# A two-headed SSM kernel: inverse transform on row halves of TensorE, final stage on two groups at once, eight skips on VectorE, and a new order

## The chip, the cores and the metric

The kernel runs on one NeuronCore of a Trainium2 chip. The metric is the device time of one launch in microseconds (us); the median of a few runs is given. PE is TensorE (matmul), PEld its weight loads, DVE is VectorE, ACT ScalarE, POOL GpSimd, and SP the engine whose queue issues most DMAs.

## The reference

Two heads work on inputs of 2048 positions and 640 channels, and their outputs stand side by side in a 2048 x 1280 result in bf16. Head A is a diagonal complex state-space recurrence, head B a gated long convolution:

```python
# head A
Lam_bar = exp(dt * Lam); B_bar = ((Lam_bar - 1) / Lam)[:, None] * Bmat
h[t] = Lam_bar * h[t-1] + B_bar @ x[t]
y = 2 * real(h @ Cmat.T) + x * Dskip
# head B
k_shift = sum over t in 0..3 of k shifted by t, times shift_k[:, t]
kv = k_shift * v
y = irfft(rfft(pad(kv)) * rfft(pad(ssm_k)))[:S] + kv * ssm_D
out = q * y
```

## The kernel before

**Head A** splits the time axis into four interleaved phases s = 0 to 3 (`NS`) of 512 positions, and the state into five blocks j (`NT`) of 128. `pe_in` multiplies the transposed input by B and adds the preceding phase's contribution through diagonal matrices (`diagL`); its result is evicted from PSUM by `ev_in`. For phase 0, DVE turns the result by tables of angles (`tabs`), runs a real scan and turns it back. The other phases follow from it by a product and two sums (`dve_mul`, `dve_next`). `pe_proj(i, s)` then multiplies 128 states by C, in two halves of 320 output columns with ten matmuls each, and adds `x * Dskip` by three more narrow matmuls against a diagonal matrix (`diagD`). There are sixteen such blocks. ACT copies each to SBUF (`act_yo`), and SP stores it. The list `SKV` could name blocks whose skip is added on DVE instead; it is empty here.

**Head B** works on five groups G of 128 channels. Per group, four taps on PE (`pe_tap`) and a product with v give kv, which goes through DRAM to be regrouped. The filter (h) and kv are each transformed by two matmul stages (`pe_s1`, `pe_s2`) with an eviction behind each. DVE multiplies the spectra (`dve_ym`, then `dve_y`, written y in the order, in two halves). `pe_inv` takes the inverse: for each of 16 frequencies four matmuls of 128 rows, 128 columns of weights and 128 moving columns. `act_zs` evicts it to `Zs`, two transposing DMAs (`turn_z`) turn that into `Zt`, and `pe_fin` makes the final stage with 32 matmuls a group, each with a full array and 64 moving columns. `dve_ob` multiplies by q in place in `qb`, and SP stores the group. The next load of q waits for that store.

The inverse is thus one of 128 points followed by one of 16:

```python
mm(o_re, lhsT=self.H[:, 0, k1, :], rhs=yre, start=True, stop=False)
mm(o_re, lhsT=self.H[:, 2, k1, :], rhs=yim, start=False, stop=True)
mm(o_im, lhsT=self.H[:, 1, k1, :], rhs=yre, start=True, stop=False)
mm(o_im, lhsT=self.H[:, 0, k1, :], rhs=yim, start=False, stop=True)
```

**What sets the order.** `make_plan` names every piece of work with its engine and its data dependencies. The string `ORDER` lists the names in the order in which they are issued; `@n` gives the PSUM slot and `!` takes the alternative engine (an eviction on DVE instead of ACT, a load on ACT's queue instead of SP's). Each engine runs its own pieces strictly in that order, and so does each DMA queue, so a DMA that waits holds up those behind it. In the names, `inv`, `zs`, `zt`, `fin`, `ob`, `od_`, `qi` are inverse, eviction, turn, final stage, product with q, store and load of q, each with its group; `p`, `yo`, `yd` are projection, copy and store.

Of the kernel before, what the change touches and what calls it, by code (L numbers as in the profile page):

```python
# [13 lines left out]
i32 = mybir.dt.int32  # L14
# [15 lines left out]
SKV = []  # L30
# [3 lines left out]

class Plan:
# [10 lines left out]
class Kernel:  # L46


    def __init__(self, ctx, tc, out, ins):
# [16 lines left out]
        t("c26", [128, 1], i32)  # L66
# [5 lines left out]
        t("bb", [128, 128], i32)  # L72
# [12 lines left out]
        for n, k in (("r_hi", 1), ("r_a", 1), ("rm", 2), ("r_k", 32), ("m_lo", 1), ("m_k1h", 1), ("m_ri", 1), ("ccol", 4),  # L85
                     ("r_ph", 64), ("m_ph", 16), ("m_t", 16)):
            t(n, [128, k], i32)
        t("r_mask", [128, 2])
        t("m_mask", [128, 4])
        t("m_aph", [128, 16], f32)  # L90
        t("r_cv", [128, 64])
        t("m_cv", [128, 16], f32)
# [9 lines left out]
        t("Mq", [128, 16, 4])  # L102
        t("G", [128, 2, 32, 64])
        t("H", [128, 3, 16, 128])
# [20 lines left out]
        t("qb", [128, 16, 128])  # L125
# [6 lines left out]
        self.Zt = self.zz[:, 4096:8192].rearrange("p (i b) -> p i b", i=32)  # L132
# [3 lines left out]
        self.tph = [flat(n).bitcast(i32).rearrange("p (q n) -> p q n", q=2) for n in (self.qb, self.kv_st)]  # L136
# [6 lines left out]
        self.diagG = self.H[:, 2].rearrange("p a b -> p (a b)")[:, 0:3 * n * 128].rearrange("p (s j d) -> p s j d", s=3, j=n)  # L143
# [46 lines left out]
    def pool_consts2(self):  # L190
        g = self.nc.gpsimd
        one = [[0, 1]]
        g.iota(self.c30[:], pattern=one, base=2 ** 30, channel_multiplier=0)
        g.iota(self.c26[:], pattern=one, base=2 ** 26, channel_multiplier=0)
        g.iota(self.ccol[:], pattern=[[1, 4]], base=0, channel_multiplier=0)
        g.iota(self.r_k[:], pattern=[[4, 32]], base=1, channel_multiplier=0)
        for r in range(2):
            g.iota(self.rm[:, r:r + 1], pattern=one, base=2 ** 30 * (1 - 3 * r), channel_multiplier=0)
        g.iota(self.m_ph[:], pattern=[[1, 16]], base=0, channel_multiplier=0)

    def pool_consts3(self):
# [5 lines left out]
        g.iota(self.bb[:], pattern=[[1, 128]], base=0, channel_multiplier=0)  # L207
# [5 lines left out]
    def dve_consts2(self):  # L213
# [7 lines left out]
        v.tensor_scalar(out=self.m_k1h[:], in0=p, scalar1=3, scalar2=2, op0=ALU.arith_shift_right, op1=ALU.logical_shift_left)  # L221
        v.tensor_scalar(out=self.m_ri[:], in0=p, scalar1=4, scalar2=2, op0=ALU.bitwise_and, op1=ALU.logical_shift_left)
# [42 lines left out]
    def pool_phases(self):  # L265
# [5 lines left out]
        g(out=self.m_t[:], in0=self.m_ph[:], in1=b(self.m_k1h[:, 0:1], 16), op=ALU.mult)  # L271
        g(out=self.m_ph[:], in0=self.m_ph[:], in1=self.m_t[:], op=ALU.add)
        g(out=self.m_ph[:], in0=self.m_ph[:], in1=b(self.m_ri[:, 0:1], 16), op=ALU.add)
        g(out=self.m_ph[:], in0=self.m_ph[:], in1=b(self.c26[:, 0:1], 16), op=ALU.mult)

    def act_RM(self):
        self.nc.scalar.activation(out=self.r_cv[:], in_=self.r_ph[:], func=ACT.Sin, scale=SC)
        self.cos(self.m_cv[:], self.m_ph[:], self.m_aph[:])

    def dve_RM(self):  # L280
# [4 lines left out]
        v.scalar_tensor_tensor(out=self.Mq[:], in0=self.m_cv[:].rearrange("p (a o) -> p a o", o=1).to_broadcast([128, 16, 4]), scalar=1.0 / L,  # L285
                               in1=self.m_mask[:].rearrange("p (o c) -> p o c", o=1).to_broadcast([128, 16, 4]), op0=ALU.mult, op1=ALU.mult)
# [13 lines left out]
    def pool_kk(self):  # L300
        g = self.nc.gpsimd.tensor_tensor
        g(out=self.kk[:], in0=self.kk[:], in1=self.hP[:, 0:1].to_broadcast([128, 16]), op=ALU.add)
        g(out=self.bb[:], in0=self.bb[:], in1=self.c19[:, 0:1].to_broadcast([128, 128]), op=ALU.mult)

    def pool_H(self, q):
        self.nc.gpsimd.tensor_tensor(
            out=self.tph[(NT + q) % 2][:, 0].rearrange("p (a b) -> p a b", a=4),
            in0=self.kk[:, 4 * q:4 * q + 4].rearrange("p (a o) -> p a o", o=1).to_broadcast([128, 4, 128]),
            in1=self.bb[:].rearrange("p (o b) -> p o b", o=1).to_broadcast([128, 4, 128]), op=ALU.mult)

    def act_H(self, q):
        v, ks = self.tph[(NT + q) % 2].rearrange("p r (a b) -> p r a b", a=4), slice(4 * q, 4 * q + 4)
        self.nc.scalar.activation(out=self.H[:, 1, ks, :], in_=v[:, 0], func=ACT.Sin, scale=SC)
        self.cos(self.H[:, 0, ks, :], v[:, 0], v[:, 1].bitcast(f32))

    def dve_nH(self):
        self.nc.vector.tensor_scalar_mul(out=self.H[:, 2], in0=self.H[:, 1], scalar1=-1.0)
# [253 lines left out]
    def pe_proj(self, i, s, ps):  # L571
# [4 lines left out]
        for b in range(2):  # L576
# [22 lines left out]
    def dve_yo(self, i, s, n, ps):  # L599
        v = lambda a: a.rearrange("q (b n) -> q b n", b=2)  # L600
        self.nc.vector.tensor_tensor(out=v(self.yo[(NS * i + s) % NY]), in0=ps[:, :, 0:320], in1=v(self.xs[n % NX]), op=ALU.add)

    def act_yo(self, i, s, ps):
        self.nc.scalar.copy(out=self.yo[(NS * i + s) % NY].rearrange("q (b n) -> q b n", b=2), in_=ps[:, :, 0:320])  # L604

    def store_yo(self, eng, i, s):
        eng.dma_start(out=self.o2[512 * i:512 * i + 512, 0:D].rearrange("(m s) d -> s m d", s=NS)[s], in_=self.yo[(NS * i + s) % NY])
# [87 lines left out]
    def pe_inv(self, ks, ps):  # L695
        mm = self.nc.tensor.matmul
        psf = ps[:].rearrange("p a n -> p (a n)")
        for i, k1 in enumerate(ks):
            yre, yim = (self.Xs[:, k1 // 8, r, 128 * (k1 % 8):128 * (k1 % 8) + 128] for r in range(2))
            o_re, o_im = psf[:, 256 * i:256 * i + 128], psf[:, 256 * i + 128:256 * i + 256]  # L700
            mm(o_re, lhsT=self.H[:, 0, k1, :], rhs=yre, start=True, stop=False)  # L701
            mm(o_re, lhsT=self.H[:, 2, k1, :], rhs=yim, start=False, stop=True)  # L702
            mm(o_im, lhsT=self.H[:, 1, k1, :], rhs=yre, start=True, stop=False)  # L703
            mm(o_im, lhsT=self.H[:, 0, k1, :], rhs=yim, start=False, stop=True)  # L704

    def act_zs(self, ks, ps):
        self.copy(self.Zs[:, :, 2 * ks[0]:2 * ks[0] + 8, :].rearrange("p i k c -> p k i c"),
                  ps[:].rearrange("p a n -> p (a n)").rearrange("p (k i c) -> p k i c", k=8, i=32))

    def turn_z(self, hf):  # L710
        s = slice(16 * hf, 16 * hf + 16)
        self.nc.sync.dma_start_transpose(out=self.Zt[:, s, :], in_=self.Zs[:, s].rearrange("p i k c -> p i (k c)"))

    def load_q(self, eng, G):
        eng.dma_start(out=self.qb[:], in_=self.q2[:, 128 * G:128 * G + 128].rearrange("(a b) c -> b a c", b=128))

    def pe_fin(self, hf, ps):
        psf = ps[:].rearrange("p a n -> p (a n)")
        for i in range(16):
            self.nc.tensor.matmul(psf[:, 64 * i:64 * i + 64], lhsT=self.Zt[:, 16 * hf + i, :],  # L720
                                  rhs=self.Mq[:].rearrange("p a c -> p (a c)"), start=True, stop=True)

    def dve_ob(self, hf, ps):
        cs = slice(64 * hf, 64 * hf + 64)
        self.nc.vector.tensor_tensor(out=self.qb[:, :, cs].rearrange("p a (i c) -> p a i c", c=4),  # L725
                                     in0=ps[:].rearrange("p a n -> p (a n)").rearrange("p (i a c) -> p a i c", i=16, a=16),
                                     in1=self.qb[:, :, cs].rearrange("p a (i c) -> p a i c", c=4), op=ALU.mult)

    def store_ob(self, eng, G):
# [303 lines left out]
```

## Time and profile before

| | us |
|---|---|
| median of 3 runs | 201.65 (201.57 to 202.29) |
| the profiled execution | 201.36 |
| its span | 199.6 |
| busy PE, DVE, ACT, POOL | 186.4, 164.9, 153.8, 24.8 |

The span runs from the first to the last instruction of the profiled execution; 1.76 us lie around it. Busy time adds what an engine spent in instructions. Matmuls are pipelined, so their records overlap, and a matmul's share of PE is the distance between two starts (its slot) rather than its recorded length. An idle time in square brackets is followed by what ended it.

### The profile page before, as it was taken

To read this page: it belongs to the slowest core of one execution; us is meant where nothing else is said; L and a number is where in the kernel's file an instruction comes from. 1 tells how busy PE (TensorE), PEld (TensorE's weight loads), DVE (VectorE), ACT (ScalarE), POOL (GpSimd) and SP (SyncE) were. 2 spreads that over 40 slices of the span, in tenths; PEclk is the share of its full clock that TensorE was granted. 3 is DMA by queue.
4 is the path that set the end of the run, shared out by engine and by line. 5 is a ranking of instruction groups with operands and counts; after the bars stand their busy time and mean duration, and the time that the engine had idled before them with its cause. 6 is when DMAs were issued, how large, how long until landed. Compare 5 with 4: busy or idle time off the path is not lost. (4 is left out here: it accounts for less than half of the span.)

```text
span 199.6 us, 7503 instructions
## 1 busy us (share of the span) xinstructions
PE 186.4 (93%) x3328; PEld 128.3 (64%) x3340; DVE 164.9 (83%) x285; ACT 153.8 (77%) x189; POOL 24.8 (12%) x55
## 2 busy tenths in 40 slices
PE   7999999999989999999999998887999999999990
PEld 4444365544445456567777887677778887977770
DVE  5899877999999999999999999999999898420040
ACT  2499999988958998899998899799898983501321
POOL 8899561000000000000000000000000000000000
PEclk9999999999999999999999999999999999999998
DMA  4999999993586831985999786997995796597635
GB/s 112 209 221 217 207 266 214 210 192 85 90 174 163 164 50 27 240 163 86 236 188 194 121 167 126 157 254 140 194 155 150 158 164 153 126 175 176 143 130 138
DMA packets 124908, 32.61 MB, mean 163 GB/s; under 512 B 120903, under 2 KB 124236, under 8 KB 124876
## 3 DMA queue, kind: packets, MB, share of 16 engines
q1 hardware_dynamic: 124856, 32.13, 81.0%
q8 instruction: 26, 0.43, 0.9%
q14 instruction: 6, 0.05, 0.1%
q10 hardware_dynamic: 20, 0.01, 0.0%
HBM read 9.51 MB, written 7.86 MB: 87 GB/s over the span
## 5 line engine op out<-in xcount | busy, mean ns | idle before, releaser
L520 PE MATMUL ps<-xT,BT 128*128 128x512 bf16 x188 | 47.8, 381 | 0.9 <-DMA xT<-in_A_x_dram 0.3
L582 PE MATMUL ps<-Cs,hs 128*128 128x320 bf16 x240 | 36.3, 299 | 0.3 <-ACT Xs L467 0.3
L520 PEld LDWEIGHTS <-BT 128*128 128x128 bf16 x200 | 18.7, 98 | 22.6 <-issue 1.3
L604 ACT CAST BT<-ps 128x640 bf16<-128x640 f32 x16 | 10.9, 695 | 25.7 <-PE ps L587 22.7
L582 PEld LDWEIGHTS <-hs 128*128 128x128 bf16 x240 | 21.9, 98 | 7.9 <-issue 0.2
L725 DVE TENSOR_TENSOR qb<-ps,qb 128x1024 bf16<-128x1024 f32 x10 | 11.9, 1216 | 15.9 <-PE ps L720 15.9
L675 PEld LDWEIGHTS <-G 128*64 128x64 bf16 x640 | 19.1, 110 | 5.5 <-issue 4.1
L467 ACT CAST As_kv<-ps 128x1024 bf16<-128x1024 f32 x20 | 20.0, 1041 | 0.3 <-PE ps L662 0.3
L467 ACT CAST As_h<-ps 128x1024 bf16<-128x1024 f32 x20 | 19.8, 1040 | 0.0
L467 ACT CAST Hf<-ps 128x1024 bf16<-128x1024 f32 x19 | 19.3, 1042 | 0.0
L467 ACT CAST Xs<-ps 128x1024 bf16<-128x1024 f32 x19 | 18.8, 1031 | 0.0
L467 ACT CAST zz<-ps 128x1024 bf16<-128x1024 f32 x17 | 17.2, 1034 | 2.1 <-PE ps L704 2.1
L701 PE MATMUL ps<-Xs,H 128*128 128x128 bf16 x80 | 17.5, 219 | 0.9 <-ACT As_h L467 0.5
L703 PE MATMUL ps<-Xs,H 128*128 128x128 bf16 x80 | 17.5, 219 | 0.8 <-issue 0.8
L702 PE MATMUL ps<-Xs,H 128*128 128x128 bf16 x80 | 17.5, 219 | 0.4 <-DVE Xs L693 0.4
L704 PE MATMUL ps<-Xs,H 128*128 128x128 bf16 x80 | 17.5, 219 | 0.0
L693 DVE TENSOR_TENSOR Xs<-Xs,rot 128x1024 bf16<-128x1024 bf16 x20 | 12.9, 686 | 0.2
L687 DVE TENSOR_TENSOR rot<-Xs,Hf 128x2048 bf16<-128x2048 bf16 x10 | 12.2, 1220 | 0.8 <-ACT BT L604 0.5
L675 PE MATMUL ps<-As_kv,G 128*64 128x128 bf16 x320 | 11.7, 221 | 1.0 <-DVE vT L651 0.5
L688 DVE TENSOR_TENSOR Xs<-Xs,Hf 128x2048 bf16<-128x2048 bf16 x10 | 12.2, 1225 | 0.5
L675 PE MATMUL ps<-As_h,G 128*64 128x128 bf16 x320 | 11.7, 221 | 0.7 <-ACT Xs L467 0.7
L651 DVE TENSOR_TENSOR vT<-ps,vT 128x1024 bf16<-128x1024 f32 x10 | 11.9, 1213 | 0.4 <-PE ps L646 0.4
(204 smaller groups left out, 396.5 us busy)
## 6 DMA issues: line engine op xcount, KB each, us to landing
h_st<-in_B_ssm_k_dram SPq DMA_DIRECT2D x10, 256.0 KB, 4.2
kv_rows<-vT SPq DMA_DIRECT2D x5, 512.0 KB
kv_st<-kv_rows SPq DMA_DIRECT2D x10, 256.0 KB, 3.7
qb<-in_B_q_dram SPq DMA_DIRECT2D x5, 512.0 KB, 4.0
out_dram<-BT SPq DMA_DIRECT2D x16, 160.0 KB, 2.6
out_dram<-qb SPq DMA_DIRECT2D x5, 512.0 KB, 5.2
As_kv<-in_A_B_re_dram SPq DMA_DIRECT2D x3, 160.0 KB, 2.4
As_kv<-in_A_B_im_dram SPq DMA_DIRECT2D x3, 160.0 KB, 2.5
```

The source lines that it names most:

```text
L467: self.nc.scalar.copy(out=out, in_=in_)
L520: mm(o, lhsT=self.BT[:, r, k, j * 128:(j + 1) * 128], rhs=xT[:, k, :], start=(k == 0), stop=(s == 1 and k == NT - 1))
L582: mm(o[:, 0:320], lhsT=h[:, r, ts], rhs=self.Cs[:, r, j, c0:c0 + 320], start=(j == 0 and r == 0), stop=(not on_pe and j == NT - 1 and r == 1))
L651: self.nc.vector.tensor_tensor(out=self.vT[:, ts], in0=ps[:].rearrange("p a n -> p (a n)"), in1=self.vT[:, ts], op=ALU.mult)
L675: self.nc.tensor.matmul(o[64 * e:64 * e + 64, c:c + 128], lhsT=self.G[:, r, k, :], rhs=As[:, k, :], start=True, stop=True)
L687: tt(out=self.cross(), in0=X[:, ::-1, :], in1=self.Hf[:, 1:2, hs].to_broadcast([128, 2, 1024]), op=ALU.mult)
L688: tt(out=X, in0=X, in1=self.Hf[:, 0:1, hs].to_broadcast([128, 2, 1024]), op=ALU.mult)
L693: self.nc.vector.tensor_tensor(out=X[:, r, :], in0=X[:, r, :], in1=cr[:, r, :], op=ALU.add if r else ALU.subtract)
L701: mm(o_re, lhsT=self.H[:, 0, k1, :], rhs=yre, start=True, stop=False)
L702: mm(o_re, lhsT=self.H[:, 2, k1, :], rhs=yim, start=False, stop=True)
L703: mm(o_im, lhsT=self.H[:, 1, k1, :], rhs=yre, start=True, stop=False)
L704: mm(o_im, lhsT=self.H[:, 0, k1, :], rhs=yim, start=False, stop=True)
```

## The change

**Inverse.** It becomes one of 64 points followed by one of 32. A matmul uses 64 rows of the array; the upper and the lower 64 rows hold the two halves e of the spectrum and write to two PSUM banks. Real and imaginary part stand side by side in the 128 columns of weights, taken from a table `H` of three strips (-sin, cos, sin) of which two neighbours are used. There are still 64 matmuls of 128 moving columns a group. The tables take two rounds on POOL and ACT instead of four. An eviction becomes two instructions of half the size.

**Final stage.** It has two weights' halves (real, imaginary) that accumulate, 64 output rows and 128 moving columns, so two groups share a PSUM tile, one in each half of the partitions: groups 0 and 1, 2 and 3, and group 4 by itself with its channels split in two. `qb` holds 64 partitions a group, and `Zt` gets a second buffer in the place of `tabs`. For group 4, q and the output move in two DMAs with rows of 64 channels instead of 128.

**Skip.** Eight of the sixteen projection blocks leave out the three skip matmuls per half. For these SP loads x, DVE multiplies it by Dskip (`skip_x`) and adds it while copying from PSUM (`dve_yo`). The last block of the old kind, (3, 3), is split into halves with a copy and a store each.

**Order.** Two of five warm-up pieces go, and the whole string `ORDER` is new.

```diff
-SKV = []
+SKV = [(2, 1), (0, 1), (2, 0), (3, 2), (2, 3), (3, 1), (1, 1), (1, 3)]
+LAST = (3, 3)
...
     def pe_inv(self, ks, ps):
...
+        for i, k1 in enumerate(ks):
+            for r in range(2):
+                for e in range(2):
+                    rows = slice(64 * e, 64 * e + 64)
+                    y = self.Xs[rows, k1 // 8, r, 128 * (k1 % 8):128 * (k1 % 8) + 128]
+                    self.nc.tensor.matmul(ps[:, e, 128 * i:128 * i + 128], lhsT=self.H[rows, k1, 1 - r:3 - r, :].rearrange("p o n -> p (o n)"),
+                                          rhs=y, start=(r == 0), stop=(r == 1))
...
+    def act_zs(self, ks, ps):
+        for e in range(2):
+            k = 16 * e + ks[0]
+            self.copy(self.Zs[:, :, k:k + 4].rearrange("p i k c -> p k i c"), ps[:, e].rearrange("p (k i c) -> p k i c", k=4, c=4))
...
+    def pe_fin(self, G, q, ps):
         psf = ps[:].rearrange("p a n -> p (a n)")
+        for i in range(8):
+            for r in range(2):
+                for h in range(2):
+                    g, j = (0, 16 * h + 8 * q + i) if G == NG - 1 else (h, 8 * q + i)
+                    self.nc.tensor.matmul(psf[64 * h:64 * h + 64, 128 * i:128 * i + 128], lhsT=self.Zt[g][:, j, 64 * r:64 * r + 64],
+                                          rhs=self.Mq[:, r].rearrange("p a c -> p (a c)"), start=(r == 0), stop=(r == 1))
...
-    for n, (w, d) in enumerate(((2, "dc"), (2, "wm0"), (2, "bt0"), (2, "bt1"), (2, "wm3"))):
+    for n, (w, d) in enumerate(((2, "dc"), (2, "wm0"), (2, "tsk"))):
...
+        old = [f"od_{x}" for x in ([G - 2, G - 1] if last else [G - 2])] if G > 1 else Hs + [f"tab{j}" for j in J]
+        dma(f"qi{G}", "SP", 0.8 if last else 0.42, 3.9 if last else 2.9, old, lambda e, G=G: K.qo(e, G, True))
...
-lv1! pc lsk lv0! lv4 B0 pc2 dc dc3 wm0@0 lv2! zer lv3! pc3 dc2 wm1@2 B1 gp1 dsel x1 tsk@4 gp0 bt0@6 tske@4 dS0 tv@0 wm2@2 pp
+lv3! pc lv4 B1 lsk lv0 pc2 dc3 lv2 lv1! B0! dc x1 zer wm0@0 gp0 dc2 wm1@2 bt1@4 gp1 tv@6 bt0@0 be1@4 kT0 pc3 tve@6 tsk@2 be0!@0
...
```

On DVE, before, the end of its work from the last group's spectra on stands as follows; `Xs<-Xs,rot` is the second half of the spectral product (y), `zz<-ps` an eviction of the inverse, `qb<-ps,qb` a product with q:

```order
L687 TENSOR_TENSOR rot<-Xs,Hf 128x2048
L688 TENSOR_TENSOR Xs<-Xs,Hf 128x2048
L693 TENSOR_TENSOR Xs<-Xs,rot 128x1024 x2
L465 CAST zz<-ps_64 128x8x32x4
L725 TENSOR_TENSOR qb<-ps_65,qb 128x16x64
L725 TENSOR_TENSOR qb<-ps_67,qb 128x16x64
```

After, the same place on DVE, where `BT<-BT` is a skip product and `BT<-ps,BT` the addition of a skip:

```order
L691 TENSOR_TENSOR rot<-Xs,Hf 128x2048
L692 TENSOR_TENSOR Xs<-Xs,Hf 128x2048
L603 TENSOR_TENSOR BT<-ps_64,BT 128x640
L697 TENSOR_TENSOR Xs<-Xs,rot 128x1024 x2
L738 TENSOR_TENSOR qb<-ps_65,qb 128x32x32
L599 TENSOR_TENSOR BT<-BT 128x640
L738 TENSOR_TENSOR qb<-ps_64,qb 128x32x32
L599 TENSOR_TENSOR BT<-BT 128x640
L738 TENSOR_TENSOR qb<-ps_65,qb 128x32x32
L738 TENSOR_TENSOR qb<-ps_67,qb 128x32x32
```

Behind the last spectral product there stood the two products of group 3; now the four of groups 2 and 3 stand there, with skip work between and behind them.

The queue of SP near its end, before; `zz<-zz` is a turn, `qb<-in_B_q` a load of q, `out_dram<-qb` the store of a group, `out_dram<-BT` that of a projection block:

```order
L715 DMA qb<-in_B_q_dram 128x16x128
L712 DMA_TRANSPOSE zz<-zz 128x16x128 x2
L730 DMA out_dram<-qb 128x16x128
L607 DMA out_dram<-BT 128x640
L715 DMA qb<-in_B_q_dram 128x16x128
L607 DMA out_dram<-BT 128x640 x5
L730 DMA out_dram<-qb 128x16x128
```

And after, where `BT<-in_A_x` loads x for a skip:

```order
L715 DMA_TRANSPOSE zz<-zz 128x16x128
L725 DMA out_dram<-qb 64x32x128 x2
L593 DMA BT<-in_A_x_dram 128x640
L715 DMA_TRANSPOSE zz<-zz 128x16x128
L723 DMA qb<-in_B_q_dram 64x32x64 x2
L611 DMA out_dram<-BT 128x320
L611 DMA out_dram<-BT 128x640
L593 DMA BT<-in_A_x_dram 128x640
```

The last load of q has moved behind the stores of two groups, a load of x and one of group 4's turns.

234 lines of the change are left out of this document (119 added, 115 removed).

## The prediction

> **What bounds the kernel now.** I read the page's busy shares and slices first, then busy time by stage, then the chain that ended last.
>
> ```profile
> span 199.6 us, 7503 instructions
> PE 186.4 (93%) x3328; PEld 128.3 (64%) x3340; DVE 164.9 (83%) x285; ACT 153.8 (77%) x189; POOL 24.8 (12%) x55
> PE   7999999999989999999999998887999999999990
> DVE  5899877999999999999999999999999898420040
> ```
>
> PE is full almost from first to last slice; DVE is as full until about 165 us and then has nearly nothing to do. The answer by stages (length, then busy time of PE, PEld, DVE, ACT, POOL) says it in numbers:
>
> ```profile
> 30.00:60.00 30.00, 29.20 (x431) 14.91 (x424) 28.41 (x46) 25.33 (x32) 0.78 (x1) 1.00 0.86 161
> 60.00:90.00 30.00, 29.26 (x550) 17.48 (x547) 29.25 (x43) 27.37 (x30) 0.00 (x0) 1.00 0.63 133
> 90.00:120.00 30.00, 29.26 (x710) 23.55 (x704) 29.48 (x51) 28.00 (x32) 0.00 (x0) 1.00 0.89 165
> 120.00:150.00 30.00, 26.61 (x787) 22.02 (x782) 29.38 (x44) 27.80 (x31) 0.00 (x0) 1.00 0.95 172
> 173.00:191.00 18.00, 18.00 (x166) 13.49 (x164) 3.02 (x3) 2.73 (x5) 0.00 (x0) 1.00 0.74 154
> ```
>
> From 60 to 150 us DVE is idle 0.75 + 0.52 + 0.62 = 1.9 us of 90, and PE 0.74 + 0.74 + 3.39 = 4.9 us. So two engines bind there together, DVE a little harder. From 173 us PE alone works, on projection blocks that were left over. The seam is the last product of the convolution's spectra on DVE (y of group 4), after which the last inverse can run:
>
> ```profile
> 168.31 1.29 DVE L693 TENSOR_TENSOR Xs<-Xs,rot 128x1024 bf16<-128x1024 bf16 x2
> 191.46 2.35 DVE L725 TENSOR_TENSOR qb<-ps,qb 128x1024 bf16<-128x1024 f32 x2 [15.44 <-PE ps L720]
> 193.84 0.38 SPq L730 DMA_DIRECT2D out_dram<-qb  x1
> 194.53 0.30 PE L587 MATMUL ps<-diagD,xT 128*128 128x64 bf16 x3
> 195.59 0.33 SPq L607 DMA_DIRECT2D out_dram<-BT  x1
> ```
>
> I call the end of y of group 4 Z: here 168.31 + 1.29 = 169.6. Behind Z come 25.1 us of PE (its last skip matmuls start at 194.53 and their slots end at 194.7) and then 4.9 us of copy and stores: Z + 30.0 = 199.6. A gain must bring Z forward or shorten what follows it. The profiled execution took 201.36, so 1.76 lie around the span; the runs' median, 201.65, is 0.3 above it.
>
> **The PE terms.** The chain that ended last gives each matmul's slot (start, then length on the chain):
>
> ```profile
> 170.21 0.06 PE ps L701
> ...
> 171.33 0.06 PE ps L701
> ...
> 172.44 0.47 PE ps L720 x16
> 172.91 1.36 PE ps L582 x10
> 174.27 0.14 PE ps L587 x3
> ```
>
> Lines 701 to 704 take turns in the inverse; between the two quoted starts of line 701 lie 20 matmuls, so 1.12 / 20 = 0.056 each, and 320 of them are 17.9 us. A final-stage matmul of 64 columns is 0.47 / 16 = 0.029: 160 make 4.7. A projection half is 1.36 and its skip 0.14, so a block is 3.00 and without skip 2.72.
>
> The inverse keeps 320 matmuls of 128 columns, but each uses 64 rows of the array, in pairs on the upper and the lower half. No row of before has that shape. Nearest is the forward second stage, in pairs on column halves, 128 columns each:
>
> ```profile
> 62.90 0.38 PE L523 MATMUL ps<-hs,diagL 128*128 128x512 bf16 x1
> 63.21 0.64 PE L675 MATMUL ps<-As_kv,G 128*64 128x128 bf16 x16
> 63.68 0.61 PE L675 MATMUL ps<-As_h,G 128*64 128x128 bf16 x16
> 64.13 0.61 PE L675 MATMUL ps<-As_kv,G 128*64 128x128 bf16 x16
> ```
>
> Sixteen take 0.45 to 0.47, so 0.0288 each. I take that: 320 x (0.056 - 0.0288) = -8.7. Ends: 0.056 (the halves don't overlap), 0.0; for a cheaper one no row speaks. The final stage goes from 160 matmuls of 64 columns to 320 of 128 columns on column halves, which is the shape just quoted: 9.2 - 4.7 = +4.5. Eight skips leave PE: 8 x 0.28 = -2.2. Sum -6.4.
>
> Both stages leave the full-array mode of the projection, so changes of mode count. The last L523 above starts at 62.90 and its 512 columns need 0.22, yet L675 starts at 63.21: 0.09 per change. In the order I count 74 changes before and 72 after, so this term is nought. [...]
>
> The start: the first projection input's transposing load is what the first large matmul waits for.
>
> ```profile
> 3.94 9.07 SPq L182 DMA_TRANSPOSE xT<-in_A_x_dram  x3
> 9.65 4.71 PE L520 MATMUL ps<-xT,BT 128*128 128x512 bf16 x19 [0.28 <-DMA xT<-in_A_x_dram]
> ```
>
> Eight issues stand ahead of it there, some 0.4 us each; after, four do, so it starts about 1.5 us earlier. PE still has to transpose two B blocks first, so I take -0.7 (0 to -1.5). Two of five warm-up pieces go; they lie ahead of that load and count nothing.
>
> **The DVE terms.** Ahead of Z the order has on DVE two final products fewer, two evictions of the recurrence and one of B fewer, and lambda and gamma go to POOL; it has one more swap of k, four skip products, three additions of the skip.
>
> ```profile
> L725 DVE TENSOR_TENSOR qb<-ps,qb 128x1024 bf16<-128x1024 f32 x10 | 11.9, 1216 | 15.9 <-PE ps L720 15.9
> L465 DVE CAST hs<-ps 128x1024 bf16<-128x1024 f32 x3 | 3.6, 1211 | 0.0
> L539 DVE TENSOR_TENSOR rot<-rot 128x512 bf16<-128x512 bf16 x10 | 3.8, 422 | 0.2
> L693 DVE TENSOR_TENSOR Xs<-Xs,rot 128x1024 bf16<-128x1024 bf16 x20 | 12.9, 686 | 0.2
> L623 DVE COPY kS<-kT 64x1032 bf16<-64x1032 bf16 x2 | 0.9, 435 | 0.1
> L380 DVE TENSOR_TENSOR lam<-rr,cos 128x5 f32<-128x5 f32 x1 | 1.0, 1005 | 0.1
> ```
>
> Removed: 2 x 1.22 + 3 x 1.21 = 6.1. Added: a swap 0.87; four products of 640 elements between 0.42 and 0.69, by length 0.49, so 2.0; three additions of 640 from PSUM below 1.22, by length 0.82, so 2.5; the rest near nothing. That is -0.7. Lambda and gamma are a dozen instructions on 5 to 15 elements, 1.0 for the row shown and some 3 in all; they stand in the first 20 us where DVE also waits, so they are worth 0 to -3. DVE thus lets Z come 0.7 to 3.7 earlier. PE work ahead of Z falls too: of the 6.4, the tail takes 3.6 (below), leaving -2.8 and the start's -0.7. I take the middle of DVE's bounds, since DVE is the fuller of the two, so Z earlier by 2.3: 167.3. Eight copies of 0.69 also leave ACT, which bounds nothing.
>
> **The tail after Z.** As the order shown with the change has it, all four final products of groups 2 and 3 have moved behind Z on DVE, with two skip products among them. On SP the last q load now stands behind the stores of two groups, whose buffer it overwrites, and behind a turn; the final products, the last store and three more stores queue behind it.
>
> ```profile
> qb<-in_B_q_dram SPq DMA_DIRECT2D x5, 512.0 KB, 4.0
> out_dram<-qb SPq DMA_DIRECT2D x5, 512.0 KB, 5.2
> ```
>
> PE after Z: two inverse pieces 0.9, two final pieces of groups 2 and 3 (32 matmuls, 0.92 each) 1.8, four blocks without skip 10.9, the split block 3.0, three mode changes 0.3: group 4's final stage may start at Z + 16.9, ends its first piece at 17.8 and its second at 18.7, and with the last block, 2.8, PE ends at Z + 21.5 (before 25.1: the 3.6 above). Data: four products and two skip products, 4 x 1.22 + 2 x 0.49 = 5.9, then the two stores. One needs 5.2; two overlapped between 5.2 and 10.4, I take 7: Z + 12.9. Then q: a second issue 0.4 and a landing of 4.0, more behind a turn, so 5.2: Z + 18.5, 0.7 later than PE needs it. Two products 2.4: Z + 20.9. From the last store's issue to the end before was 199.6 - 193.84 = 5.8; after it is two DMAs with rows of half the length, twice as many, so 0.4 + 0.8 more (0 to 2.6 for the rows): Z + 27.9.
>
> Sum: 167.3 + 27.9 = 195.2; with the 1.76 around the span and the median's 0.3, 197.3.
>
> **Rivals.**
> - PE alone decides: q lands in time and DVE keeps up. Then PE ends at 194.7 - 6.4 - 0.7 = 187.6; the final stage is through 2.8 before that, its last product 1.5 later, and the store then needs 7.0: 193.3, so with the 1.76 and 0.3 195.4. For it: PE's share. Against it: the two stores ahead of q. Decides if these land within 6 us.
> - Z stays: DVE, full already, gains nothing from a shorter PE, so 169.6 + 27.9 = 197.5, so 199.6. For it: DVE's idle of 1.9 in 90; against: the work taken off DVE and PE ahead of Z.
> - Slower: the row halves do not overlap, because each half loads its own 128 columns of weights. Price: the inverse keeps 0.056 a matmul, 8.7 over the PE sum: 195.4 + 8.7 = 204.1. It turns slower than before from 0.048 a matmul (195.4 + 320 x 0.0195 = 201.65). Against it speaks the first stage, four quarter tiles, each matmul with its own load:
>
> ```profile
> 108.81 0.44 PE L662 MATMUL ps<-R,h_st 64*64 64x64 bf16 x32
> 109.08 0.76 PE L662 MATMUL ps<-R,kv_st 64*64 64x64 bf16 x64
> ```
>
> There 32 matmuls and 32 loads of 64 columns fit into 0.27. [...]
>
> **How the numbers follow.** Forecast (q late) 0.45; PE alone 0.22; Z stays 0.16; halves serial 0.09; 0.08 for an order that loses more in waits than it gains in PE, half of it near no change. The range runs from PE alone with 3 us less of waits, 192.4, to Z stays with 1.2 more for the stores, 200.8. Faster by over 0.5% (about what a measurement of this kernel can tell from no change, 1.0 us) takes the first two and nearly all of the third: 0.80; within it 0.07; slower 0.13.
>
> **What would show it.** Inverse matmuls 0.029 apart; final pieces of 32 in 0.92; Z near 167; the final product of group 4 waiting for the q load rather than for PE; last store issued some 7 us before the end. Wrong if the inverse pieces take 0.9, if Z is at 169 or later, or if PE has more than 8 us of waits from 60 us on.

## The result, and the profile after

The changed kernel takes 212.05 us (median of 4, 208.60 to 213.41) against 201.69 (201.57 to 202.29): ratio 1.040, 95% interval 1.029 to 1.051. It is slower; the prediction was 197.3. Its executions scatter (their mean granted PE clocks are 0.972 to 0.989), and each ratio here leaves out those that stand apart as slow (of the changed kernel, two of four). The profiled execution took 211.06, its span is 209.3.

The page after: span and busy times, busy slices, and the queue named "instruction".

```profile
span 209.3 us, 7744 instructions
PE 181.9 (87%) x3433; PEld 121.0 (58%) x3448; DVE 172.1 (82%) x288; ACT 147.2 (70%) x194; POOL 25.4 (12%) x66
PE   5399999899999999997899999888778996999930
DVE  4099889999999999999999999978799779930460
q8 instruction: 27, 0.44, 1.0%
```

PE is busy 4.5 us less in a span 9.7 us longer. The first two columns and those from 120 us on are thinner in PE and in DVE. By stages (columns as before: length, busy PE, PEld, DVE, ACT, POOL, clock, DMA share, GB/s), after first and then before; the last row of each runs from the start to Z:

```profile
0.00:10.00 10.00, 4.05 (x24) 2.46 (x25) 2.64 (x25) 2.62 (x3) 7.10 (x30) 1.00 0.89 160
120.00:150.00 30.00, 27.47 (x766) 21.76 (x759) 27.53 (x44) 27.47 (x35) 0.00 (x0) 1.00 0.89 173
150.00:178.20 28.20, 23.06 (x647) 18.27 (x642) 23.71 (x29) 19.77 (x26) 0.00 (x0) 1.00 1.02 172
0.00:178.20 178.20, 160.14 (x3149) 104.56 (x3165) 159.05 (x273) 144.55 (x189) 25.39 (x66) 1.00 0.90 165
```

```profile
0.00:10.00 10.00, 8.38 (x44) 4.47 (x45) 7.31 (x48) 3.77 (x5) 8.37 (x32) 1.00 0.69 161
150.00:169.60 19.60, 18.94 (x444) 16.20 (x443) 17.68 (x21) 14.63 (x18) 0.00 (x0) 1.00 0.75 157
0.00:169.60 169.60, 161.19 (x3051) 108.60 (x3064) 159.04 (x280) 146.50 (x180) 24.79 (x55) 1.00 0.85 166
```

Up to Z, DVE works 159.05 us against 159.04: the same. What grew is its idle time, 10.6 to 19.2 us, and Z moved by exactly that, from 169.6 to 178.2. So the question is who made DVE wait. The rows of the program's start, of the places where PE stood, and of the tail (timelines of PE, DVE and SP; a bracket tells the idle time ahead and its releaser):

```profile
5.43 0.71 PE L487 MATMUL ps<-ident,As_kv 128*128 128x128 bf16 x5
9.68 0.72 PE L487 MATMUL ps<-ident,As_kv 128*128 128x128 bf16 x5 [3.54 <-DMA As_kv<-in_A_B_im_dram]
12.24 1.06 PE L522 MATMUL ps<-xT,BT 128*128 128x512 bf16 x2
141.90 0.27 PE L705 MATMUL ps<-Xs,H 64*128 64x128 bf16 x3 [0.28 <-issue]
155.01 0.22 PE L666 MATMUL ps<-R,h_st 64*64 64x64 bf16 x3 [1.54 <-issue]
158.89 1.07 PE L705 MATMUL ps<-Xs,H 64*128 64x128 bf16 x32
195.59 1.98 PE L733 MATMUL ps<-Mq,zz 128*64 128x128 bf16 x64 [0.28 <-DMA zz<-zz]
```

```profile
176.89 1.28 DVE L697 TENSOR_TENSOR Xs<-Xs,rot 128x1024 bf16<-128x1024 bf16 x2
193.36 0.49 DVE L599 TENSOR_TENSOR BT<-BT 128x640 bf16<-128x640 bf16 x1 [7.11 <-DMA BT<-in_A_x_dram]
200.72 2.36 DVE L738 TENSOR_TENSOR qb<-ps,qb 128x1024 bf16<-128x1024 f32 x2 [4.48 <-DMA qb<-in_B_q_dram]
```

```profile
183.75 3.14 SPq L725 DMA_DIRECT2D out_dram<-qb  x2
186.99 3.31 SPq L593 DMA_DIRECT2D BT<-in_A_x_dram  x1
190.40 3.44 SPq L715 DMA_TRANSPOSE zz<-zz  x1
193.93 1.98 SPq L723 DMA_DIRECT2D qb<-in_B_q_dram  x2
203.11 1.71 SPq L725 DMA_DIRECT2D out_dram<-qb  x2
```

The start: up to 9.68 PE has nothing for 3.5 us, because half of a B block has not landed; the first large matmul comes at 12.24 instead of 9.65. The middle: ahead of 141.90 and of 155.01 PE stands *inside* a piece, waiting for nothing the profile knows ("issue"). The tail: four items on SP's queue take 3.1, 3.3, 3.4 and 2.0 us to issue, and the final product of group 4 waits for q.

### The profile page after: what moved, and what is told of

Read it like the earlier page. It is cut to its first block, busy times and chain, and to the rows that moved or that the text cites. A ratio compares the mean times of both kernels' runs of the same rounds, so it can differ in the third digit from the quotient of the medians.

```text
span 209.3 us, 7744 instructions
## 1 busy us (share of the span) xinstructions
PE 181.9 (87%) x3433; PEld 121.0 (58%) x3448; DVE 172.1 (82%) x288; ACT 147.2 (70%) x194; POOL 25.4 (12%) x66
## 5 line engine op out<-in xcount | busy, mean ns | idle before, releaser
L522 PE MATMUL ps<-xT,BT 128*128 128x512 bf16 x185 | 49.6, 394 | 1.1 <-issue 0.4
L584 PE MATMUL ps<-Cs,hs 128*128 128x320 bf16 x240 | 35.4, 299 | 0.3 <-ACT Xs L469 0.3
L522 PEld LDWEIGHTS <-BT 128*128 128x128 bf16 x200 | 19.3, 101 | 23.7 <-issue 3.9
L584 PEld LDWEIGHTS <-hs 128*128 128x128 bf16 x240 | 22.4, 98 | 8.8 <-issue 0.3
L469 ACT CAST zz<-ps 128x512 bf16<-128x512 f32 x36 | 18.6, 615 | 6.9 <-DMA tabs<-zz 6.5
L679 PEld LDWEIGHTS <-G 128*64 128x64 bf16 x640 | 19.2, 110 | 6.5 <-issue 6.0
L469 ACT CAST BT<-ps 128x640 bf16<-128x640 f32 (+3 forms) x12 | 8.9, 772 | 13.6 <-PE ps L589 13.6
L691 DVE TENSOR_TENSOR rot<-Xs,Hf 128x2048 bf16<-128x2048 bf16 x10 | 12.2, 1222 | 0.6 <-ACT Xs L469 0.2
L692 DVE TENSOR_TENSOR Xs<-Xs,Hf 128x2048 bf16<-128x2048 bf16 x10 | 12.2, 1225 | 0.4
L705 PE MATMUL ps<-Xs,H 64*128 64x128 bf16 x320 | 11.6, 217 | 1.0 <-issue 0.6
L599 DVE TENSOR_TENSOR BT<-BT 128x640 bf16<-128x640 bf16 x8 | 3.9, 488 | 10.0 <-DMA BT<-in_A_x_dram 9.9
L733 PE MATMUL ps<-Mq,zz 128*64 128x128 bf16 x192 | 10.5, 220 | 1.8 <-DVE BT L603 1.4
L584 PE MATMUL ps<-Cs,h 128*128 128x320 bf16 x80 | 12.0, 299 | 0.1
```

Of the source, the lines that this page charges most:

```text
L469: self.nc.scalar.copy(out=out, in_=in_)
L522: mm(o, lhsT=self.BT[:, r, k, j * 128:(j + 1) * 128], rhs=xT[:, k, :], start=(k == 0), stop=(s == 1 and k == NT - 1))
L584: mm(o[:, 0:320], lhsT=h[:, r, ts], rhs=self.Cs[:, r, j, c0:c0 + 320], start=(j == 0 and r == 0), stop=(not on_pe and j == NT - 1 and r == 1))
L599: self.nc.vector.tensor_tensor(out=self.xs[n % NX], in0=self.xs[n % NX], in1=self.Db, op=ALU.mult)
L679: self.nc.tensor.matmul(o[64 * e:64 * e + 64, c:c + 128], lhsT=self.G[:, r, k, :], rhs=As[:, k, :], start=True, stop=True)
L691: tt(out=self.cross(), in0=X[:, ::-1, :], in1=self.Hf[:, 1:2, hs].to_broadcast([128, 2, 1024]), op=ALU.mult)
```

## Experiments

### The start

**e1_start**: the load of the B block (two issues, one a half) goes back to SP's queue, ahead of x.

```diff
-... lsk lv0 pc2 dc3 lv2 lv1! B0! dc x1 ...
+... lsk lv0 pc2 dc3 lv2 lv1! B0 dc x1 ...
```

> The changed kernel with one move: the load of B0 goes back from ACT's queue to SP's, ahead of the first transposing load of x. Theory start: PE's idle stretch from 5.9 to 9.7 us goes, the first large matmul starts at about 9.5 instead of 12.2 and the clock is full by 11 instead of 17.1 us, so the median falls by 4 to 5 us, to about 207. Rival (the middle decides, and DVE's later waits absorb an early start): the first large matmul is early too, but the span moves by less than 1.5 us.

209.73 us, ratio 1.040 (1.039 to 1.042). The first large matmul moved from 12.24 to 9.21, but Z only from 178.2 to 177.5, and the ratio is the changed kernel's. In this execution PE's clock fell to half for 3.4 us at 154.6, which it did not in the profiled execution of the changed kernel; what else takes the early start's gain isn't shown.

**e4_warm**: ten warm-up matmuls in the gap at 5.9 to 9.7 us, meant to have the clock full earlier than in the changed kernel (17.1 us; its large matmuls start 0.43 us apart ahead of that and 0.22 behind it).

```diff
-    ... enumerate(((2, "dc"), (2, "wm0"), (2, "tsk"))):
+    ... enumerate(((2, "dc"), (2, "wm0"), (10, "wm1"))):
```

> The changed kernel with ten instead of two dummy matmuls in the last warm-up piece, moved into PE's idle stretch ahead of the second B transposes; nothing else. Theory start, second half (the clock is held low because PE idled): the first large matmul still starts at about 12.2 us, but its slots are 0.216 instead of 0.427, and the median falls by about 2 us. Rival (the clock's rise has a fixed time after launch, warm-ups count nothing): slots stay at 0.427 up to 17 us and the time does not move.

211.98 us, ratio 1.050 (1.046 to 1.053): no gain. The clock was full from 8.3 us, but fell to half again for 3.4 us at 11.7.

**e7_bstart**: the kernel before with the changed start alone.

```diff
-lv1! pc lsk lv0! lv4 B0 pc2 dc dc3 wm0@0 lv2! zer lv3! pc3 dc2 wm1@2 B1 gp1 dsel x1 ...
+lv1! pc lsk lv0 lv4 B0 pc2 dc dc3 wm0@0 lv2 zer lv3 pc3 dc2 wm1@2 B1! gp1 dsel x1 ...
```

> The kernel before with the changed kernel's start alone: the second half of the first B load goes to ACT's queue, behind the first transposing load of x, and this load goes out earlier on SP. Theory 'the start is lost and stays lost': the first large matmul moves from 9.65 to about 12 us, Z from 169.6 to 173 or later, time 204.5 to 207. Rival 'absorbed' (as e1_start suggested, where a start 3 us earlier moved Z by 0.6 only): the start is late by as much, but Z moves by under 1.5 us and the time is 201.5 to 203.5.

204.36 us, ratio 1.013 (1.011 to 1.015), so +2.7 us; Z at 172.75. PE's timeline shows the same hole:

```profile
9.76 0.71 PE L485 MATMUL ps<-ident,As_kv 128*128 128x128 bf16 x5 [2.38 <-DMA As_kv<-in_A_B_im_dram]
11.97 2.34 PE L520 MATMUL ps<-xT,BT 128*128 128x512 bf16 x5
```

In a kernel that is otherwise intact the loss stays: 2.3 us at the first large matmul, 3.2 at Z.

### The skip, q and the transfers

**e3_noskip**: the changed kernel with the skip back on PE and without loads of x.

```diff
-SKV = [(2, 1), (0, 1), (2, 0), (3, 2), (2, 3), (3, 1), (1, 1), (1, 3)]
+SKV = []
```

> The changed kernel with all sixteen skips on PE again (no x loads, no skip products, copies on ACT). Theory skip traffic: eight loads of 160 KB less, DVE's 9.9 us of waits for x go, and the median falls by 3 to 6 us although PE gets 2.2 us of matmuls back. Rival (PE bounds, the x loads are hidden): slower by about 2 us, median about 214.

211.23 us, ratio 1.047 (1.044 to 1.051). Z came at 175.4, 2.8 earlier, PE's end at 202.2, 1.8 later. Ahead of Z, DVE had waited 2.8 us for a load of x; PE got the skips back. The intervals of the two ratios overlap: about an even trade.

**e15_bskip**: the kernel before with five late skips on DVE.

```diff
-SKV = []
+SKV = [(1, 1), (2, 1), (2, 3), (3, 1), (3, 3)]
...
+ Db xs1_1 xs2_1 xs2_3 behind qi3; xs3_1 behind qi4; xs3_3 behind yo2_1
```

> The kernel before with the skip of five late projection blocks on DVE (three with their x loaded behind the fourth q load, two behind the fifth), nothing else. Theory 'PE sets the tail and DVE is idle there': PE loses 5 x 0.28 = 1.4 us, Z stays, time 200.0 to 200.8. Rival 'the loads of x cost more' (SP's queue behind Z holds the last q load and the stores): 201.5 to 203.5, with the last final products waiting for q or for DVE's skip work.

205.89 us, ratio 1.022 (1.019 to 1.025). DVE's timeline shows why:

```profile
190.58 0.49 DVE L597 TENSOR_TENSOR BT<-BT 128x640 bf16<-128x640 bf16 x1 [4.70 <-DMA BT<-in_A_x_dram]
190.99 1.55 DVE L601 TENSOR_TENSOR BT<-ps,BT 128x640 bf16<-128x640 f32 x2
194.24 0.49 DVE L597 TENSOR_TENSOR BT<-BT 128x640 bf16<-128x640 bf16 x1 [1.70 <-DMA BT<-in_A_x_dram]
```

The product waits in DVE's order for its x, the copies out of PSUM stand behind it, and PE waits 2.3 and 1.4 us for these copies; at 193.3 its clock falls to half for 6.8 us. 1.4 us saved on PE cost 4.3. At this placement of the loads, the skip on DVE does not pay even alone.

**e2_q4**: a buffer of its own for group 4's q, loaded right behind group 2's.

```diff
+        self.q4 = self.vT[:].rearrange("p (a c) -> p a c", a=32)
-... qi2 ... (qi4 behind zt4_0)
+... qi2 qi4 ...
```

> The changed kernel with a buffer of its own for the q of group 4 (the place of vT, free by then), so that its load can be issued early and waits for no store. Theory q queue: DVE's wait of 4.5 us for q goes and the two loads and stores that stood behind q in SP's queue start earlier; the end of the span comes 3 to 5 us earlier, median about 208. Rival (the transfers are late because the DMA engines are full, whatever the queue's order): DVE's last products wait for the turn or for the x loads instead, and less than 1.5 us is won.

216.78 us (212.76 to 216.99). The product no longer waits for q, but Z came at 182.1, and ACT waited 12.2 us for a turn, against 6.5 in the changed kernel. Its executions had mean clocks of 0.949 to 0.958, the changed kernel's 0.972 to 0.989, so this run gives no price for the wait for q. That the load only moved into a more crowded stage is argued, not shown.

**e5_qlate**: e1_start with the q loads of groups 0 and 1 moved out of the crowd at 43 to 51 us, behind `kT2`.

> The changed kernel with its B half back on SP's queue (as in e1_start), and the q loads of groups 0 and 1 moved from the crowded 43 to 51 us to right behind kT of group 2. Theory 'DMA crowding' (q loads with twice the packet time stand ahead of the recurrence's loads, and DVE waits for these): DVE's idle of 3.7 us in 30 to 60 us falls to 2 or less, Z moves 1 to 2 us forward from e1's 177.5, and the time falls to 206 to 208.5. Rival 'the order itself' (Z is late because many small waits of DVE on PE are laid out badly from 60 us on): idle in 30 to 60 us falls but returns later; Z stays at 177 or later and the time within 1 us of e1's 209.7.

218.94 us, ratio 1.087 (1.083 to 1.091), a miss by 10 us. The two loads now stood ahead of the next kv loads, and PE waited for these 8.4 us in four waits, up to 5.2 us at a time:

```profile
PE ps L666 <- DMA kv_st<-kv_rows: 8.4, 4, 5.2
```

**e6_bsplit**: the kernel before with q and output in two DMAs of 64 partitions a group.

```diff
-        eng.dma_start(out=self.qb[:], in_=...)
+        for h in (slice(0, 64), slice(64, 128)):
+            eng.dma_start(out=self.qb[h], in_=d[h])
```

> The kernel before with each group's q load and its store split into two DMAs of 64 partitions and 16 rows each: the same bytes and packets, ten more issues, nothing else. If issues on SP's queue are what slows the changed kernel (its loads and stores of 64 partitions take about twice as long to issue), this costs 1 to 3 us: 202.5 to 204.5. If it is the packets' time or the order of the work, it costs next to nothing: 201.2 to 202.2, with Z within 0.5 us of 169.6.

202.48 us, ratio 1.005 (1.002 to 1.007), Z at 169.2. Ten more issues cost 0.9 us, none of it ahead of Z. On the order of before, the form of the transfers is a small part.

### The new arithmetic on the old order

**e8_old**: inverse and final stage as changed; start, skips and order of before, with the final pieces moved to where both groups are ready.

> The changed kernel's arithmetic (inverse as 64 and 32 points on row halves, last stage on two groups at once) on the order, the start and the skips of the kernel before; only the final stage's pieces are moved, to where the second group of a pair is ready. Theory 'the order loses it': PE gains 8.7 - 4.5 = 4.2 us, Z comes at 167 to 170 as in the kernel before, its DVE idle before Z is about 11 us as there, and the time is 196 to 200. Rival 'the arithmetic's layout loses it' (loads and stores of 64 partitions, larger packets' time, final products in pairs): Z stays at 173 or later, idle of DVE before Z is 15 us or more, and the time is 203 to 207.

214.54 us, ratio 1.067 (1.061 to 1.073). The theory that the new order loses the time falls: on the old one the new arithmetic is slower still. Of the 13.2 us that the span grew, 6.0 lie ahead of Z (175.6 instead of 169.6) and 7.2 behind it (37.2 instead of 30.0). The last product starts at Z + 28.2, where before it started at Z + 21.9, and what it waits for is q, whose load stands behind the stores of groups 2 and 3 (DVE's timeline):

```profile
203.79 2.36 DVE L738 TENSOR_TENSOR qb<-ps,qb 128x1024 bf16<-128x1024 f32 x2 [14.52 <-DMA qb<-in_B_q_dram]
```

So with this order the pairing has a price of its own. **e9_unpair** takes the pairing away too: each group has its own final stage, at before's places. Its 32 output rows are split over the two column halves, which makes 640 final matmuls of 64 columns where the changed kernel has 320 of 128.

```diff
-    g, j = (0, 16 * h + 8 * q + i) if G == NG - 1 else (h, 8 * q + i)
-    matmul(psf[64 * h:64 * h + 64, 128 * i:128 * i + 128], lhsT=self.Zt[g][:, j, ...], rhs=Mq, ...)
+    matmul(psf[64 * h:64 * h + 64, 64 * i:64 * i + 64], lhsT=self.Zt[0][:, 16 * hf + i, ...], rhs=Mq[:, 64 * h:64 * h + 64], ...)
```

> The changed kernel's inverse (64 and 32 points on row halves) on the order, start and skips of the kernel before, with a final stage that doesn't pair groups: each group by itself, its 32 output rows split over the two column halves, so that its first piece needs only the first half of the turn and stands in the order exactly where it stood before; q and the output move in two DMAs of 64 partitions a group (as in e6_bsplit). PE's work is that of the changed kernel within 0.5 us. Theory 'pairing' (the waits of PE and DVE in the changed kernel and in e8_old come from final stages that need both groups' turns and then put four products in a row on DVE): PE's waits fall from e8's 24.7 to 12 or less, Z to 167 to 170, and the time to 197 to 201. Rival 'inverse' (the eviction in two instructions, the whole spectrum half per bank, or the 64-row mode itself bring the waits): Z stays at 173 or later and the time at 205 or more.

212.19 us, ratio 1.051 (1.049 to 1.052). This doesn't clear the pairing: e9 has 3808 matmuls, 320 more than e8 and 480 more than before, so one cost was traded for another. Up to the third group's spectra (134.2 us) e9 runs level with before (134.1); from there it falls behind, and PE's timeline has rows like these:

```profile
131.67 0.31 PE L666 MATMUL ps<-R,kv_st 64*64 64x64 bf16 x14
134.59 0.34 PE L666 MATMUL ps<-R,kv_st 64*64 64x64 bf16 x18 [2.61 <-issue]
```

Fourteen of 32 like matmuls, then 2.6 us of nothing, then the rest. The piece had begun, so I take its data to be there and its place in PSUM to be its own. What can be missing, then, is the instruction itself. The page of before counts 3328 matmuls and 3340 loads, 6668, and 26 packets of 16 KB on the queue "instruction": 256 a packet; after, 6881 in 27, 255. The stops inside a piece that the profile calls "issue", of 0.25 us or more, from 60 us on, beside the packets of that queue and the matmuls and loads counted in the trace:

```
kernel     PE goes on   stood us    16 KB packet had   matmuls and loads
           at us        ("issue")   landed us before   since the stop above
changed    141.90       0.28        1.66               -
           151.00       0.85        1.81               512
           155.01       1.54        1.38               256
           163.29       0.36        1.31               512
e9_unpair  118.71       1.27        1.54               -
           134.59       2.61        1.38               767
           139.14       1.53        1.27               256
           154.93       1.59        1.44               767
e8_old     132.60       2.45        1.58               -
before     135.29       0.82        1.34               -
```

Within one row, all stops of a kernel lie whole multiples of 256 rows apart, and each ends 1.3 to 1.8 us after a packet of that queue has landed. Together they are 7.0 us in e9, 3.0 in the changed kernel, 2.45 in e8 and 0.8 in the kernel before. In e9, from 100 us on, the packet behind a border starts mostly 1.0 to 2.8 us after PE has passed it, and takes 0.9 to 1.6. From these, with the 1.3 to 1.8 us above, I estimate some 4 us for a block to come; PE would stand where it uses up 256 instructions sooner. The shortest times in which PE passed 256 rows, counted on from the first stop above, are 3.7 us in the changed kernel and 3.9 in the one before. Of e8's 13 us its one stop is a small part; the rest of what e8 loses ahead of Z was not taken apart. PE's clock fell in two of these kernels too: ahead of Z it stood at half for 10.2 us in e9's profiled execution, for 3.4 in e8's, and not at all from 20 us on in before's or the changed kernel's.

### Instructions against columns

**e10_split**: the kernel before, each inverse matmul as two of 64 columns.

```diff
+            for c in (0, 64):
-            mm(o_re, lhsT=self.H[:, 0, k1, :], rhs=yre, start=True, stop=False)
+                        self.nc.tensor.matmul(psf[:, 256 * i + o + c:256 * i + o + c + 64], lhsT=..., rhs=y[r], ...)
```

> The kernel before, with each inverse matmul of 128 columns made two of 64 columns with the same weights: the same columns, so the same array time by the final stage's row (16 of 64 columns in 0.47), but 320 matmuls and 320 weight loads more, all in the dense stages. Theory 'instruction fetch' (PE gets its instructions in blocks of 16 KB, about 256 rows of the trace each, and cannot pass a block's border sooner than about 4.2 us after the border before it): 640 instructions more are 2.5 blocks; PE stalls inside pieces, each stall ending some 1.4 us after the landing of a 16 KB packet, and the time rises by 4 to 10 us, to 205 to 212. Rival 'array' (only columns and modes count): within 1 us of 201.6, and no stalls inside pieces.

206.58 us, ratio 1.023 (1.020 to 1.027), Z at 174.4; the waits and the timeline of PE:

```profile
PE ps L662 <- issue: 3.2, 2, 1.8
135.31 0.22 PE L662 MATMUL ps<-R,h_st 64*64 64x64 bf16 x2 [1.79 <-issue]
135.45 2.04 PE L702 MATMUL ps<-Xs,H 128*128 128x64 bf16 x64
```

Two stops of that kind, 3.2 us in all, 767 rows apart, have taken the place of the one of 0.8: 2.4 us more. The columns weren't quite free: 64 in 2.04, less 0.2 for the last one's own record (0.19 for 64 columns at line 720 of before), are 0.029 each, so a pair takes 0.058 instead of 0.056, some 0.7 us over 320. Right behind the second stop, at 150.7, the clock fell to half for 3.4 us in which PE was busy throughout; I estimate up to 1.7 for that, half of its length. Together these come to 4.8, by which Z moved; that they simply add up is argued. More instructions at almost the same columns made a kernel that has none of the change slower by 2.3%.

**e11_halfcols** and **e12_halfinstr**: the changed kernel with half of the columns, and with half of the matmuls, of inverse and final stage.

```diff
-  y = self.Xs[rows, k1 // 8, r, ... + 128]      # e11: and as much in pe_fin
+  y = self.Xs[rows, k1 // 8, r, ... + 64]
-            for r in range(2):                   # e12: in pe_inv and pe_fin
+            for r in range(1):
```

> The changed kernel, with inverse and final stage leaving out half of their columns (64 of 128 a matmul): the number of PE's instructions stays, the array time of the two stages falls from about 18.5 to about 9.2 us if columns set it. The left-out half is whatever the buffer held before. Theory 'instruction fetch': block borders in the dense stages stay about 4.2 us apart, Z and the time move by under 2 us (210 to 213). Theory 'array': PE has 9 us less to do, and the time falls by 4 or more, to 208 or less.

> The changed kernel, with inverse and final stage leaving out their imaginary parts: half of their matmuls and loads (640 instructions, 2.5 blocks), each with its full 128 columns, so the same 9.2 us of array time goes as in e11_halfcols. Theory 'instruction fetch': no stall inside pieces is left or nearly none, Z moves forward by 3 us or more, and the time is 4 us or more below that of e11_halfcols, at 202 to 207. Theory 'array': the same time as e11_halfcols within 1 us.

212.26 us, ratio 1.041 (1.034 to 1.047), and 209.88, ratio 1.039 (1.034 to 1.044). By the starts of their matmuls, each of the two takes some 7.5 us off PE's time in the two stages. Half of the columns bring nothing, as the fetch theory has it, but half of the instructions bring nothing that the intervals can tell either, against it. PE's time in these stages is thus not what the changed kernel waits for. In e12 the waits that the profile calls "issue" fell from 3.7 us to 1.7, but in their place PE waited longer (4.0 us instead of 1.5) for the convolution's kv, loaded back from DRAM:

```profile
PE ps L666 <- DMA kv_st<-kv_rows: 4.0, 3, 2.0
```

In the changed kernel the fetch is therefore not the only limit. **e13_oldinstr** and **e14_oldcols** repeat the pair on e9_unpair, where start, skips and order are those of before.

> e9_unpair (the new inverse and an unpaired final stage on the order of before) leaving out the imaginary parts of both: half of their matmuls and loads. PE then has as many matmuls as the kernel before (3328) and about 8 us less array time. Theory 'instruction fetch': no stalls inside pieces beyond before's, Z at 167 to 170.5, time 197 to 203, 9 us or more below e9's 212.2. Rival 'something else in the new stages' (evictions in two instructions, DMAs of 64 partitions, 64-row mode): Z at 174 or later, time 206 or more.

> e9_unpair leaving out half of the columns of each matmul of inverse and final stage: as much array time goes as in e13_oldinstr, all instructions stay. Theory 'instruction fetch': stalls inside pieces stay, Z at 175 or later, time 207 to 213. Theory 'array': the time of e13_oldinstr within 1.5 us.

Half of the instructions: 205.92 us (204.30 to 206.72, and one execution of 591.93 that nothing on record explains), ratio 1.019 (1.013 to 1.025), Z at 172.2, not one stop inside a piece. Half of the columns: 210.79, ratio 1.044 (1.040 to 1.047), stops of 1.4 to 1.8 us inside pieces as in e9; the execution profiled took 215.11, with Z at 179.3 and the clock at half for 20.5 us ahead of it. But the two did not take as much array time off. A final piece in PE's timelines of e9, of e14 and of e13:

```profile
170.07 1.21 PE L732 MATMUL ps<-Mq,zz 128*64 128x64 bf16 x64
169.13 1.16 PE L732 MATMUL ps<-Mq,zz 128*64 128x32 bf16 x64
170.68 0.69 PE L732 MATMUL ps<-Mq,zz 128*64 128x64 bf16 x32
```

At 32 columns the 64 matmuls took 1.16 us against 1.21 at 64 columns, and half as many took 0.69. By their starts, e14 freed about 3.5 us of PE's time in the two stages, and e13 about 9.4. The 4.9 us between the two runs can thus be the 5.9 us of PE's time as well as the 960 instructions by which they differ, and this pair doesn't settle what the fetch costs. What speaks for the fetch on the old order is e10, and that e13 has no stop where e9 has 7.0 us of them. The 1.9% that e13 still lacks weren't taken apart; its inverse pieces wait for evictions, and its clock falls to half twice, for 10.2 us in all.

**e16_three**: the changed kernel with e1's start, without skips on DVE, and with e12's half of instructions.

> The changed kernel with three things taken out at once: its B half back on SP's queue (e1_start), no skip on DVE (e3_noskip), and inverse and final stage without their imaginary parts (e12_halfinstr, half of their instructions). Alone these gave back 2.3, 0.8 and 2.2 us. Theory 'each adds its own': 212.05 - 5.3 = 206.8, so 206 to 208. Theory 'one limit behind the other': more than the sum, 201 to 205.5. Rival 'the new order itself': less than the sum, 208 or more, with PE waiting for the recurrence's loads (kv_st) and Z at 174 or later.

207.88 us, ratio 1.032 (1.030 to 1.033). The 2.3, 0.8 and 2.2 us of the expectation are differences of medians; by the ratios (1.040, 1.047 and 1.039) none of the three alone is told apart from the changed kernel (1.029 to 1.051), and neither are all together. So this run doesn't decide between the theories. Most of the loss is still there, and PE's largest wait in it is again for the convolution's kv (the expectation calls these the recurrence's loads):

```profile
PE ps L666 <- DMA kv_st<-kv_rows: 5.3, 4, 1.9
```

No kernel here beats the one before.

## Why the prediction was wrong

- **Inverse 0.029 a matmul: right.** 32 took 1.07 us at 158.89, less 0.2 for the last one's own record (0.22) 0.027 each. So the row halves overlapped (0.027 against 0.056 before), and that rival was rightly held small. **Final stage +4.5: right** (64 in 1.98 less 0.2: 0.028). PE's busy time fell by 4.5 us.
- **"Z earlier by 2.3: 167.3": the step that failed.** Z came at 178.2, which is 10.9 of the 14.1 us between forecast (195.2) and span (209.3). I let Z follow DVE's work, 0.7 to 3.7 us less, and took DVE's idle time ahead of Z as unchanged, without a reason. The work stayed at 159.0, 2.3 more than I had taken, and the idle time grew by 8.6: by 4.7 in the first 10 us (2.7 to 7.4), by 1.9 at 120 to 150 and by 2.6 behind, with 0.5 less between. In the last stretch lie a wait for x of 2.8 and PE's stops of 0.85, 1.54 and 0.36. The three additions and four products were costed by length; their loads were not costed at all. How the 8.6 us divide among start, loads and stops stays open, since undoing these one by one moved the time by nothing that the intervals can tell.
- **"The start -0.7": wrong by 3.3 us at the first large matmul**, which came 2.6 later. I took four issues ahead of the load of x off the sum and did not ask where they had gone. Two of them, the halves of a B block, went to ACT's queue, and the second was issued behind the first transposing load. e7 puts this at +2.7 us for the whole kernel of before; e1 shows the changed kernel to give back little of it. That the warm-up pieces count nothing is not contradicted: e4's ten more matmuls brought no gain.
- **"Sum -6.4" counted columns, and no term stood for the instructions.** A matmul and its load are two instructions, in before 256 of these go to one packet of the queue "instruction", and the stages were already the densest of the program. The inverse kept its 640 instructions in half the time, and the final stage went from 320 to 640. e10 shows the price on the kernel before. In the changed kernel the stops came to 3.0 us instead of 0.8: a part of what Z lost, and not the whole. The traces of before had it: PE's count in the first part of the page, the queue "instruction" in the third, and one wait for nothing, 0.8 us, among PE's waits. None was read.
- **The tail, Z + 27.9: Z + 31.1.** Stores issued at Z + 5.6 (forecast 5.9), PE ended at Z + 22.2 (21.5): right. The likeliest case, q late, was right as a mechanism: the last product waited 4.5 us for q. But it began at Z + 22.5 instead of 18.5. I held the load back by the landing of the two stores; SP spent 3.1 + 3.3 + 3.4 us on issuing the stores, a load of x and a turn, in order, and the load of q came fourth.
- **The rivals.** "Z stays" was too mild. The slower case, with 0.13 in all, named row halves, which do overlap. Nearest in kind was the 0.08 for an order that loses more in waits than it gains in PE; it named no wait and had no size. Two bounds that I had set as wrong were reached: Z at 169 or later, and more than 8 us of PE's waits from 60 us on (PE was idle for 10.7 us from there to Z, against 5.5 before).
- **The order.** On the old order the parts cost 1.3% (start), 2.2% (five skips, at places of their own) and 6.7% (arithmetic, paired; 5.1% unpaired, with more matmuls), and all of them together 4.0% on the new one. So each part loses where it was tried alone, and the new order seems to make good part of it. The parts were tried apart, and their sum is argued, not shown.

## What to carry to other kernels

Before you shorten matmuls, divide PE's instructions by the packets on the page's instruction queue, and ask how soon a block of 256 is used up: where that is near the 4 us estimated here, shorter matmuls may only bring PE to the next stop sooner. When an experiment takes half of something away, read from its trace what it really took: e14's halved columns left the final stage as long as it was. When an engine's work is unchanged, its idle time is the result; forecast that, wait by wait, and not the work. A load that leaves a queue goes somewhere: cost it at the place where it now stands.

## What the runs showed of the hardware

- **A queue named "instruction" moved packets of 16 KB while the program ran**: 26 in the kernel before and 27 in the changed one, one per 256 and 255 matmuls and loads. At the stops in the table PE went on 1.3 to 1.8 us after one of them had landed, and it stood in the middle of a piece for up to 2.6 us (e9). That these packets hold PE's instructions is my conclusion from the counts and the stops; no view shows what is in them.
- **A load on ACT's queue came late beside a transposing load on SP's.** The second half of the B block was issued on ACT's queue at 3.17 us, 0.7 after the transposing load on SP, and PE could use it at 9.68. In the kernel before it was issued at 3.46 on SP, ahead of the transposing load, and PE used its block from 6.39 on. Which of the two delays it, the other queue or the transposing load, no run tells apart; in e7 the first half, issued on ACT's queue 0.6 after the transposing load, was in use at 6.66, and the second, issued 0.4 later, at 9.76.
- **PE's clock fell to half in the middle of some runs.** In before it stands at 1.00 from 30 to 197.9 us. In e13 it stood at 0.50 from 119.0 to 122.3 us and from 156.4 to 163.2, in e9 from 140.5 to 143.8 and from 154.1 to 160.9. By stages of e13 (columns as above):

```profile
150.00:156.40 6.40, 3.65 (x150) 2.83 (x148) 4.75 (x9) 5.13 (x7) 0.00 (x0) 1.00 0.85 207
153.00:156.40 3.40, 1.20 (x24) 0.85 (x24) 1.78 (x3) 2.63 (x5) 0.00 (x0) 1.00 0.50 146
156.40:163.20 6.80, 6.05 (x164) 5.92 (x165) 4.25 (x6) 4.76 (x7) 0.00 (x0) 0.50 0.80 140
```

In the 3.4 us just ahead PE was busy 35% of the time (1.20 of 3.40), in three short pieces with pauses between, and then had half its clock for 6.8 us. PE's idle time alone doesn't tell when the clock falls: in the changed kernel PE was idle for 10.7 us from 60 us to Z, and its clock stood at 1.00 all the while. What sets it, no run here shows.
